# A pair's check numbers on GpSimd: in the step of the pair's last threshold instead of four steps later

## The chip, the cores and the metric

The kernel runs on one core of a Trainium2 chip. The metric is the device time of one execution in microseconds (us). The kernel before has a median of 878.46 us; the execution that was profiled took 872.71 us, of which its trace spans 870.8 us.

## The reference

Sparse attention, then a soft mixture of experts, then a two-layer MLP. Only the first part is touched. For each of 4 batches and 8 heads (sequence 576, head dimension 64) a row of scores keeps its 32 largest values:

```python
scores = scale * np.matmul(q, k.transpose(0, 1, 3, 2))
kth = np.partition(scores, -top_k, axis=-1)[..., -top_k:-top_k + 1]
mask = scores >= kth
scores = np.where(mask, scores, -1000000000.0)
scores = scores - np.max(scores, axis=-1, keepdims=True)
attn = np.exp(scores)
attn = attn / (np.sum(attn, axis=-1, keepdims=True) + 1e-09)
return np.matmul(attn, v).astype(np.float32)
```

Its output is the input of the experts, and theirs of the MLP. In the kernel these are three stages one behind the other.

## The kernel before

**Pairs, tiles and steps.** Two heads make a pair, 16 pairs in all, numbered i from 0. A pair has 9 tiles of 128 rows of scores. A step (`step(m)`) works on two tiles, so a pair lasts 4.5 steps and the stage 72 steps; odd pairs begin in the middle of a step. All engines run the stage in an order written by hand: the string `ORDER` lists tokens, each token takes the next entry of its list, and what a step leaves in its lists is issued at its end in the order `t u U H L a p q r c w e v d m D Z`.

**What a step does.** TensorE computes the scores of step m+2 (token a, L223), ScalarE copies them to the tile x (c, L433). VectorE halves the rows of step m+1 with maxima and minima (`tree1`, token t: L238, L239, L240), and GpSimd does the missing minima as two integer operations (u and U: L246, L250). VectorE takes the 32 largest values of each row of step m by four rounds of the eight largest (`tree2`, token d: L260 and L264 three times, L267 at the end). They go into `m8`, in the trace called m: one tile for a pair, 9 x 32 values in each partition, from a pool of two buffers. So the first L260 of pair i+2 writes where pair i's values were, and must wait until every reader of pair i's tile is through. ScalarE makes a penalty R from the threshold (r, L280), TensorE adds it to the transposed scores (w, L315, L316, L320), ScalarE takes the exponentials E (e, L321), and TensorE multiplies them with the values one step later (v, L326). Row sums, reciprocals rc (L340, VectorE) and the normalised tile xl (L345, ScalarE) follow. GpSimd adds the logits of a head (`add_logits`, token l, L361 or L363), and for each coming pair it makes the low parts of q and of k (`split_lo`, token L, L161, the tiles rawq and rawk), one of them in each of two successive steps.

**The check numbers.** The halving can lose one of the 32. So for every row three of the values are compared with the 32nd (the tile cert, L465), and at the end of attention the least of all differences decides whether the program is run once more without halving. In the kernel before, L465 stands in `ending`, token l, four steps after the step with the pair's last tile and behind the addition of the logits of the pair's second head. GpSimd runs its queue in order.

Of the kernel before, what the change touches and what calls it, by code (L numbers as in the profile page):

```python
# [18 lines left out]
ALU = mybir.AluOpType  # L19
# [70 lines left out]
class Attention:  # L90
# [324 lines left out]
    def run(self, between=None):  # L415
        nc = self.nc
# [3 lines left out]
        Ds, X, Fs, m8, xls, avs, RR, ended, mxs, exs = {}, {}, {}, {}, {}, {}, {}, {}, {}, {}  # L420
# [6 lines left out]
        def at(m, token, f):  # L427
            todo[max(m, -2 if token == "Z" else -1)].append((token, f))

        def copy(m, ps, u, hf):  # L430
            if m not in X:
                X[m] = self.tree.tile([128, 2, 576], F32, name="x", bufs=XBUFS)
            nc.scalar.copy(X[m][:, u, 288 * hf : 288 * hf + 288], ps)  # L433

        def relu(n):
            m, t = m8[seq[n][0]], seq[n][1]
            if n < 2 * M - 2:
                R = RR[seq[n]] = self.w3.tile([128, 576], BF16, name="R", bufs=RB)
                self.relu(R, X[n // 2][:, n % 2], m, t)
            else:  # L440

                if not spare:
                    spare.append(self.w2.tile([128, 5, 2, 97], F32, name="V").rearrange("p a b c -> p (a b c)").bitcast(BF16))
                R = RR[seq[n]] = spare[0][:, 576 * (n % 2) : 576 * (n % 2) + 576]
                nc.vector.tensor_scalar(R, X[n // 2][:, n % 2], m[:, t, 31:32], None, ALU.is_lt)

        def values(ex, i, g, slot):

            h = g[0]
            if i not in xls:  # L450
                xls[i] = self.w3.tile([128, 5, 2, 96], F32, name="xl", bufs=XL)
                nc.gpsimd.memset(xls[i][96:128, 2:5], -1e30)
            if (i, h) not in avs:
                avs[i, h] = self.pA.tile([128, 5, 97], F32, name="av")
            self.values(slot, ex, Ds[i]["V"], h, avs[i, h])

        def ending(i, h):

            if (i, h) != (npairs - 1, 1):
                self.add_logits(i, h, xls[i])  # L460
            if h == 0:
                return
            if self.fast:

                nc.gpsimd.tensor_tensor(self.k.cert[:, i], m8[i].rearrange("p t (j e) -> p t j e", e=8)[:, :, 0:3, 7],  # L465
                                        m8[i][:, :, 31:32].to_broadcast([128, 9, 3]), op=ALU.subtract)
            if i % NPAIR == NPAIR - 1:
                sides["x"][0].append((0, self.route(i // NPAIR, [xls[i - 3 + p] for p in range(NPAIR)])))

        def side(name, m, engine):  # L470

            wait, now = sides[name]
            if not now and wait and wait[0][0] <= m:
                g = wait.pop(0)[1]
                now += [g, next(g)]
            if now and engine in (now[1], None):
                now[1] = next(now[0], "")
                if not now[1]:
                    now.clear()

        def step(m):
            nonlocal idle
            if m == M:
                idle = self.pS.tile([128, 288], F32, name="s")
            q = collections.defaultdict(list, carry)
            carry.clear()

            def add(token, f):
                q[token].append(f)

            if 0 <= m + 2 < M:
                scored = []
                for u in range(2):
                    for hf in range(2):
                        add("a", lambda n=seq[2 * m + 4 + u], u=u, hf=hf: scored.append((self.scores(*n, hf), u, hf)))
                        add("c", lambda: copy(m + 2, *scored.pop(0)))
            if 0 <= m + 1 < M:
                up = self.tree1(X[m + 1], m < 0)
                add("t", lambda: Fs.update({m + 1: next(up)}))
                add("u", lambda: next(up, None))  # L500
                add("U", lambda: next(up, None))
            for n in (2 * m - 2, 2 * m - 1):
                if 0 <= n < 2 * M:
                    add("r", lambda n=n: relu(n))
            if m - 1 in ended:

                i, g = ended[m - 1]
                ex, pms, exps = [], [], []
                exs[m - 1] = ex
                add("p", lambda: pms.append(self.maxima_rows(g, mxs.pop(m - 1))))  # L510
                add("q", lambda: self.maxima_copy(g, pms.pop()))

                def weights(cs):
                    if not ex:
                        ex.append(self.w2.tile([128, 5, 320], F32, name="E"))
                    exps.append(self.weights(i, g, {u: RR[i, u] for u in g[1]}, ex[0], cs))

                for cs in [[0, 1], [2, 3], [4]] if g[4] == 256 else [[0], [1], [2], [3], [4]]:
                    add("w", lambda cs=cs: weights(cs))
                    add("e", lambda: exps.pop(0)())  # L520
            if m - 2 in ended:

                iv, gv = ended[m - 2]
                for slot in IN_GROUP[gv[4]]:
                    add("v", lambda slot=slot: values(exs[m - 2][0], iv, gv, slot))
                if gv[1][-1] in (4, 8):

                    key, rs, rc = (iv, gv[0]), [], []
                    at(m + 1, "s", lambda: rs.append(self.sums(avs[key], key[1], m > M)))
                    at(m + 1, "i", lambda: rc.append(self.recip(rs[0])))  # L530
                    if m > M:
                        at(m + 1, "i", lambda: self.last_logits(avs[key], rc[0], iv))
                    for t in range(5):
                        at(m + 1, "n", lambda t=t: self.normalize(avs[key], rc[0], xls[key[0]], key[1], t))
                    at(m + 2, "l", lambda: ending(*key))
            if m in ended:
                add("m", lambda: mxs.update({m: self.maxima(m8[ended[m][0]], ended[m][1])}))
            if 0 <= m < M:
                ms = []
                for n in (2 * m, 2 * m + 1):  # L540
                    i_, t = seq[n]
                    if t == 0:
                        m8[i_] = self.w2.tile([128, 9, 32], F32, name="m8")
                    ms.append(m8[i_][:, t])
                tr = self.tree2(Fs.pop(m), ms)
                for _ in range(5):
                    add("d", lambda: next(tr, None))
            for token, f in todo.pop(m, []):
                add(token, f)
            for name in (ORDER if m < M else END).split():  # L550
                if name[0] == "k":

                    for _ in range(int(name[1:])):
                        self.nc.tensor.matmul(idle[:, :256], self.k.idn.bitcast(BF16)[:, :128], self.k.idn.bitcast(BF16), start=True, stop=True)
                elif name[0] in sides:
                    side(name[0], m, name[1])
                elif q[name]:
                    q[name].pop(0)()
            for name in "t u U H L a p q r c w e v d m D Z".split():
                while q[name]:  # L560
                    q[name].pop(0)()
            carry.update({name: fs for name, fs in q.items() if fs})
            if between:
                between(m)
# [18 lines left out]
        with self.tc.manual_schedule(engines={ENG.Activation, ENG.PE, ENG.DVE, ENG.Pool, ENG.SP}):  # L583
# [17 lines left out]
            for m in range(-2, M + 4):  # L601
                step(m)
# [450 lines left out]
```

## Time and profile before

| | |
|---|---|
| median of the runs | 878.46 us (fastest 878.17) |
| the profiled execution | 872.71 us, span 870.8 us |
| busy, share of the span | TensorE 88%, VectorE 85%, ScalarE 68%, GpSimd 48% |
| steps of attention in full run | about 35 to 505 us |
| tail of attention, experts | about 505 to 600 us |
| MLP | about 600 to 871 us |

Busy shares are means over three stages with different limits, and a busy TensorE includes matmuls whose ends are modelled. For a change in one stage, the idle time of each engine inside that stage and what ended it tell more than the shares.

### The profile page before, as it was taken

How to read it: one execution, taken by the hardware profiler on the slowest of the kernel's cores; microseconds unless marked ns; L12 is line 12 of the kernel's file. 1: busy time of each engine (PE TensorE's matmuls, PEld its weight loads, DVE VectorE, ACT ScalarE, POOL GpSimd, SP SyncE). 2: the span in 40 equal slices, each digit the busy share in tenths (PEclk: the TensorE clock that was granted, in tenths of full speed). 3: DMA queues.
4: the chain of work that ended last, by engine and by line, in shares of the span. 5: the costliest groups of instructions: out<-in, count | busy, mean ns of one | idle time of the engine just before them, and what ended most of it. 6: DMA issues, size and time to landing. Idle time of an engine off the chain costs nothing.

```text
span 870.8 us, 17807 instructions
## 1 busy us (share of the span) xinstructions
PE 766.0 (88%) x6222; PEld 659.8 (76%) x6222; DVE 736.7 (85%) x2206; ACT 593.8 (68%) x1330; POOL 419.0 (48%) x475
## 2 busy tenths in 40 slices
PE   4689999989989999899999898895479889999997
PEld 2588898889878889798898776672357667888885
DVE  3998988998898998889988946768989998868773
ACT  3478888878877888778778753227665755676562
POOL 3466566556576556565556520002635453433432
PEclk7699999999999999999999999996889999999999
DMA  3626446634654665365153468991130000001011
GB/s 86 160 71 169 120 106 162 165 83 130 160 125 117 178 143 146 104 165 124 41 131 87 149 236 334 404 383 49 57 136 1 1 36 37 1 0 73 1 38 41
DMA packets 60985, 103.41 MB, mean 119 GB/s; under 512 B 24853, under 2 KB 24853, under 8 KB 59861
## 3 DMA queue, kind: packets, MB, share of 16 engines
q1 hardware_dynamic: 60884, 102.18, 40.3%
q8 instruction: 51, 0.84, 0.4%
q14 instruction: 50, 0.40, 0.2%
HBM read 69.86 MB, written 4.72 MB: 86 GB/s over the span
## 4 chain that ended last, share of the span: by engine, by line
PE 39%; DVE 38%; ACT 7%; POOL 5%; issue 5%; DMA 4%; SPq 1%; POOLq 0%; DVEq 0%; ACTq 0%
DVE f L264 7%; PE av L326 7%; DVE m L260 6%; PE o L971 5%; PE o L972 5%; PE o L973 5%; DVE m L267 4%; DVE h L238 4%; DVE hs L944 3%; DVE e L937 2%; DVE f L239 2%; PE s L223 2%; DVE hs L935 2%; PE st L315 2%; DVE f L240 2%
## 5 line engine op out<-in xcount | busy, mean ns | idle before, releaser
L326 PE MATMUL av<-V,E 112*107 112x97 f32 (+5 forms) x1600 | 190.9, 267 | 1.6 <-ACT E L321 1.6
L246 POOL TENSOR_TENSOR f<-x,h 128x576 int32<-128x576 int32 x71 | 100.5, 1416 | 167.2 <-DVE f L240 68.1
L326 PEld LDWEIGHTS av<-V,E 112*107 112x107 f32 (+5 forms) x1600 | 177.2, 181 | 1.8 <-ACT E L321 1.7
L1007 ACT ACTIVATE e<-e 128x768 f32<-128x768 f32 (+2 forms) x168 | 115.3, 744 | 74.8 <-DVE e L937 74.5
L321 ACT ACTIVATE E<-st 128x320 f32<-128x320 f32 (+2 forms) x256 | 117.5, 487 | 55.4 <-PE st L320 52.4
L947 POOL TENSOR_TENSOR gl<-hs,gh 128x768 fp32r<-128x768 f32 (+2 forms) x56 | 92.6, 1654 | 128.0 <-DVE gh L946 123.8
L260 DVE MAX8 m<-f 128x8 f32<-128x100 f32 (+2 forms) x432 | 119.4, 316 | 33.3 <-POOL cert L465 33.3
L264 DVE MATCH_REPLACE8 f<-m,f 128x100 f32<-128x100 f32 (+2 forms) x432 | 131.5, 312 | 0.0
L315 PE MATMUL st<-Qs,Ka 128*128 128x256 f32 (+1 forms) x320 | 110.2, 352 | 14.5 <-ACT E L321 14.1
L223 PE MATMUL s<-Ka,Qs 128*128 128x288 f32 x320 | 104.8, 341 | 18.0 <-ACT Ka L186 9.9
L972 PE MATMUL o<-w,gl 128*128 128x512 f32 x288 | 117.7, 409 | 0.8 <-POOL gl L947 0.8
L971 PE MATMUL o<-w,gh 128*128 128x512 f32 x288 | 118.0, 410 | 0.0
L973 PE MATMUL o<-w,gh 128*128 128x512 f32 x288 | 117.0, 406 | 0.0
L280 ACT ACTIVATE R<-x,m 128x576 bf16<-128x576 f32 x142 | 111.7, 794 | 2.2 <-DVE m L267 0.6
L433 ACT COPY x<-s 128x288 f32<-128x288 f32 x288 | 101.7, 407 | 8.1 <-PE s L223 7.2
L250 POOL TENSOR_TENSOR f<-f,x 128x576 int32<-128x576 int32 x71 | 100.7, 1418 | 0.6
L267 DVE MAX8 m<-f 128x8 f32<-128x576 f32 x144 | 100.8, 742 | 0.0
L316 PE MATMUL st<-Qb,Kb 128*128 128x256 f32 (+1 forms) x320 | 93.9, 302 | 3.5 <-ACT Qb L305 3.5
L223 PE MATMUL s<-Kb,Qs 96*128 96x288 f32 x320 | 94.0, 308 | 0.3 <-DVE Kb L189 0.3
L320 PE MATMUL st<-dm,R 128*128 128x128 bf16 (+1 forms) x790 | 88.9, 219 | 5.1 <-ACT R L280 4.2
L223 PEld LDWEIGHTS s<-Ka,Qs 128*128 128x128 f32 x320 | 63.7, 199 | 20.4 <-ACT Ka L186 10.4
L315 PEld LDWEIGHTS st<-Qs,Ka 128*128 128x128 f32 x320 | 61.8, 193 | 19.5 <-ACT E L321 16.9
(152 smaller groups left out, 1424.9 us busy)
## 6 DMA issues: line engine op xcount, KB each, us to landing
w<-in_w SPq DMA_DIRECT2D x30, 1024.0 KB, 7.6
Ka<-hik SPq DMA_DIRECT2D x62, 144.0 KB, 2.6
raw<-in_w_in SPq DMA_DIRECT2D x8, 1024.0 KB, 8.3
raw<-in_w_out SPq DMA_DIRECT2D x8, 1024.0 KB, 5.0
rawq<-in_qT SPq DMA_DIRECT2D x16, 288.0 KB, 3.6
rawk<-in_kT SPq DMA_DIRECT2D x16, 288.0 KB, 3.3
vT<-in_vT SPq DMA_DIRECT2D x16, 288.0 KB, 4.2
Qb<-Qs SPq DMA_DIRECT2D x32, 144.0 KB, 2.6
```

Of the source, the lines that this page charges most:

```text
L223: nc.tensor.matmul(ps, q, k, start=n == 0, stop=n == len(todo) - 1)
L260: V.max(M[j][u], f[:, u, part])
L264: V.match_replace(out=f[:, u, part], in_to_replace=M[j][u], in_values=f[:, u, part], imm_value=NEG)
L267: V.max(M[3][u], f[:, u])
L280: self.nc.scalar.activation(R, x, AF.Relu, bias=m8[:, t, 31:32], scale=-1.0)
L315: T.matmul(ps[:, j], self.Ka[z][:, ks], self.Qs[z][:, 64 * h + q0 : 64 * h + q0 + n], start=j == 0, stop=False, skip_group_check=True)
L321: return lambda: nc.scalar.activation(ex[:, cs[0] : cs[0] + len(cs), :n], ps, AF.Exp, scale=SCALE)
L326: self.nc.tensor.matmul(av[:w, j], ex[:k, c, o : o + w], V[:k, c, h], start=c == 0 and j == 2 * h, stop=c == 4, skip_group_check=True)
L971: T.matmul(ps, gh[:, c, r : r + 128], w[0], start=f == 0, stop=False)
L972: T.matmul(ps, gl[:, c, r : r + 128], w[0], start=False, stop=False)
L973: T.matmul(ps, gh[:, c, r : r + 128], w[1], start=False, stop=f == 15)
L1007: nc.scalar.activation(mid[i][1], mid[i][1], func, **kw)
```

## The change

L465 moves out of `ending` into a function of its own, and that is called under the token U in the step where the pair's last tile (tile 8) gets its values. Its list of U holds the second integer operation L250 ahead of it, so it is issued at the end of the step, behind L250. The operation, its operands and its result are the same.

```diff
             if h == 0:
                 return
-            if self.fast:
-
-                nc.gpsimd.tensor_tensor(self.k.cert[:, i], m8[i].rearrange("p t (j e) -> p t j e", e=8)[:, :, 0:3, 7],
-                                        m8[i][:, :, 31:32].to_broadcast([128, 9, 3]), op=ALU.subtract)
             if i % NPAIR == NPAIR - 1:
                 sides["x"][0].append((0, self.route(i // NPAIR, [xls[i - 3 + p] for p in range(NPAIR)])))
+
+        def certify(i):
+
+            nc.gpsimd.tensor_tensor(self.k.cert[:, i], m8[i].rearrange("p t (j e) -> p t j e", e=8)[:, :, 0:3, 7],
+                                    m8[i][:, :, 31:32].to_broadcast([128, 9, 3]), op=ALU.subtract)
@@
             if m in ended:
                 add("m", lambda: mxs.update({m: self.maxima(m8[ended[m][0]], ended[m][1])}))
+                if self.fast and ended[m][1][1][-1] == 8:
+                    add("U", lambda: certify(ended[m][0]))
```

The first place is GpSimd's queue in the step where pair 4's check numbers stood; m_2070 is the tile m of pair 4, m_2460 that of pair 5. Before:

```order
L246 TENSOR_TENSOR f<-x,h 128x2x288
L291 TENSOR_SCALAR mx<-col 128x2
L292 TENSOR_TENSOR mx<-col,mx 128x2
L250 TENSOR_TENSOR f<-f,x 128x2x288
L363 TENSOR_TENSOR L<-xl 128x160
L465 TENSOR_TENSOR cert<-m_2070 128x27
L161 TENSOR_TENSOR rawq<-rawq,hiq 128x576
L246 TENSOR_TENSOR f<-x,h 128x2x288
```

And of the change:

```order
L246 TENSOR_TENSOR f<-x,h 128x2x288
L291 TENSOR_SCALAR mx<-col 128x2
L292 TENSOR_TENSOR mx<-col,mx 128x2
L250 TENSOR_TENSOR f<-f,x 128x2x288
L363 TENSOR_TENSOR L<-xl 128x160
L468 TENSOR_TENSOR cert<-m_2460 128x27
L161 TENSOR_TENSOR rawq<-rawq,hiq 128x576
L246 TENSOR_TENSOR f<-x,h 128x2x288
```

A cert still stands here, but it is that of pair 5, whose last tile falls into this step; pair 4's has gone four steps ahead. The second place is that earlier step on GpSimd, where pair 4 gets its last values (m_2071 is now the name of its tile). Before:

```order
L246 TENSOR_TENSOR f<-x,h 128x2x288
L291 TENSOR_SCALAR mx<-col 128x2
L292 TENSOR_TENSOR mx<-col,mx 128x2
L250 TENSOR_TENSOR f<-f,x 128x2x288
L161 TENSOR_TENSOR rawq<-rawq,hiq 128x576
L246 TENSOR_TENSOR f<-x,h 128x2x288
```

And of the change:

```order
L246 TENSOR_TENSOR f<-x,h 128x2x288
L291 TENSOR_SCALAR mx<-col 128x2
L292 TENSOR_TENSOR mx<-col,mx 128x2
L250 TENSOR_TENSOR f<-f,x 128x2x288
L468 TENSOR_TENSOR cert<-m_2071 128x27
L161 TENSOR_TENSOR rawq<-rawq,hiq 128x576
L246 TENSOR_TENSOR f<-x,h 128x2x288
```

The check numbers now stand ahead of the subtraction rawq of that step. The third place is VectorE, with what each instruction waits for, where pair 6 (m_3061, now m_3062) begins in the buffer of pair 4. Before:

```order
L267 MAX m_2460<-f 128x8 [waits Pool_49]
L267 MAX m_2460<-f 128x8
L290 TENSOR_REDUCE col<-m_2460 128x2
L260 MAX m_3061<-f 128x8 [waits DVE_49,Pool_49]
L260 MAX m_3061<-f 128x8
L264 MATCH_REPLACE f<-m_3061,f 128x100 [waits DVE_49] x2
```

And of the change:

```order
L267 MAX m_2460<-f 128x8 [waits Pool_49]
L267 MAX m_2460<-f 128x8
L290 TENSOR_REDUCE col<-m_2460 128x2
L260 MAX m_3062<-f 128x8 [waits DVE_49]
L260 MAX m_3062<-f 128x8
L264 MATCH_REPLACE f<-m_3062,f 128x100 [waits DVE_49] x2
```

The first L260 of the pair no longer waits for GpSimd (Pool). The orders of TensorE, ScalarE, VectorE and of the DMA queue are otherwise as before.

## Rows read from the trace of the kernel before

**Rows 1.** The page: busy time of each engine; the chain that ended last.

```profile
PE 766.0 (88%) x6222; PEld 659.8 (76%) x6222; DVE 736.7 (85%) x2206; ACT 593.8 (68%) x1330; POOL 419.0 (48%) x475
...
PE 39%; DVE 38%; ACT 7%; POOL 5%; issue 5%; DMA 4%; SPq 1%; POOLq 0%; DVEq 0%; ACTq 0%
```

**Rows 2.** Stretches: length, busy us of PE, PEld, DVE, ACT, POOL; clock, DMA.

```profile
35.00:505.00 470.00, 435.74 (x3997) 400.51 (x3997) 433.60 (x1721) 380.38 (x1012) 282.63 (x360) 0.99 0.50 128
80.00:120.00 40.00, 38.16 (x322) 35.03 (x321) 34.56 (x141) 30.88 (x83) 24.44 (x32) 0.91 0.48 130
```

**Rows 3.** Waits of VectorE, 35 to 505: total us, times, longest us.

```profile
DVE m L260 <- POOL cert L465: 33.3, 14, 2.7
DVE rc L340 <- ACT rs L335: 0.5, 1, 0.5
```

**Rows 4.** Timeline of GpSimd where pair 4's check numbers stand: start, us.

```profile
204.24 1.41 POOL L250 TENSOR_TENSOR f<-f,x 128x576 int32<-128x576 int32 x1
205.61 0.53 POOL L363 TENSOR_TENSOR L<-xl 128x160 f32<-128x160 f32 x1
206.09 0.27 POOL L465 TENSOR_TENSOR cert<-m 128x27 f32<-128x27 f32 x1
206.32 1.42 POOL L161 TENSOR_TENSOR rawq<-rawq,hiq 128x576 f32<-128x576 f32 x1
```

**Rows 5.** Timeline of VectorE at the same place.

```profile
206.40 0.43 DVE L260 MAX8 m<-f 128x8 f32<-128x100 f32 x2 [2.73 <-POOL cert L465]
...
209.57 0.75 DVE L238 TENSOR_TENSOR h<-x 128x576 f32<-128x576 f32 x1
```

**Rows 6.** Timeline of VectorE: the wait for an odd pair, two kinds.

```profile
171.95 0.27 DVE L260 MAX8 m<-f 128x8 f32<-128x100 f32 x1 [1.33 <-POOL cert L465]
...
233.75 0.27 DVE L260 MAX8 m<-f 128x8 f32<-128x100 f32 x1 [2.56 <-POOL cert L465]
```

**Rows 7.** Check numbers over the run: ns min/median/max, first and last start.

```profile
L465 POOL TENSOR_TENSOR cert<-m x16: 255/261/274, 83.8 to 519.1; 128x27 f32<-128x27 f32 x16
```

**Rows 8.** Timeline of GpSimd: two subtractions of low parts.

```profile
64.91 1.42 POOL L161 TENSOR_TENSOR rawk<-rawk,hik 128x576 f32<-128x576 f32 x1
...
119.46 1.43 POOL L161 TENSOR_TENSOR rawq<-rawq,hiq 128x576 f32<-128x576 f32 x1
```

**Rows 9.** Timeline of VectorE: the halving beside those two.

```profile
65.67 1.27 DVE L238 TENSOR_TENSOR h<-x 128x576 f32<-128x576 f32 x1
...
120.56 0.94 DVE L238 TENSOR_TENSOR h<-x 128x576 f32<-128x576 f32 x1
```

**Rows 10.** Waits of TensorE, 35 to 505.

```profile
PE st L315 <- ACT E L321: 14.1, 10, 2.5
PE m L301 <- POOL mx L292: 8.4, 10, 2.5
PE st L320 <- ACT R L280: 3.9, 15, 0.3
```

**Rows 11.** Timeline of VectorE, then ScalarE, then TensorE, 356 to 370.

```profile
356.83 0.27 DVE L260 MAX8 m<-f 128x8 f32<-128x100 f32 x1 [2.55 <-POOL cert L465]
...
367.62 0.18 DVE L340 RECIPROCAL rc<-rs 128x5 f32<-128x5 f32 x1
...
367.84 0.34 ACT L345 ACTIVATE xl<-av,rc 128x96 f32<-128x96 f32 x1 [2.83 <-DVE rc L340]
...
369.62 0.38 PE L315 MATMUL st<-Qs,Ka 128*128 128x256 f32 x1 [2.51 <-ACT E L321]
```

**Rows 12.** Timeline of ScalarE and VectorE: a copy of scores, the halving that reads it.

```profile
396.81 0.99 ACT L433 COPY x<-s 128x288 f32<-128x288 f32 x3
...
399.65 0.92 DVE L238 TENSOR_TENSOR h<-x 128x576 f32<-128x576 f32 x1
```

**Rows 13.** Timeline of TensorE: ten values matmuls at the two clock levels.

```profile
365.98 1.13 PE L326 MATMUL av<-V,E 112*107 112x97 f32 x10
...
371.38 2.28 PE L326 MATMUL av<-V,E 112*128 112x97 f32 x10
```

## The prediction

> **What bounds the kernel now.** I read the page first. TensorE and VectorE are both above 80% busy and share the chain that ended last almost evenly [rows 1], so over the whole span neither is the bound. The change touches attention alone, so I then read the stretch of full steps, 35 to 505 us: TensorE is busy 435.7, VectorE 433.6 and ScalarE 380.4 of 470 us [rows 2]. Two engines have the same 35 us left. The waits tell which of them is driven. VectorE waits for one thing only: 14 times for the check numbers, 33.3 us in all; everything else adds 0.5 us [rows 3]. So VectorE never ran out of scores, and outside these 14 waits it is gapless. The 14 are the pairs 2 to 15, each waiting for the cert of the pair two before it.
>
> The place of the wait shows the mechanism. GpSimd finishes L250, adds the logits, takes the check numbers at 206.09 to 206.36 [rows 4], and VectorE's first L260 of the next pair starts at 206.40 after 2.73 us of idling [rows 5]. The cert itself takes 0.26 us [rows 7]; what VectorE waits for is the queue ahead of it. All 7 even pairs (their certs stand behind a pair with L363 or L361 and before a rawq) look like this place and cost about 2.73. The 7 odd pairs come in two kinds, 2.56 and 1.33 us [rows 6]; the short one is the end of a batch, where VectorE adds the logits itself: 3 of the 7. 7 x 2.73 + 4 x 2.56 + 3 x 1.33 = 33.3, the sum of the waits row.
>
> **What the change removes.** The new cert stands one pair-length of 4.5 steps ahead of the L260 that needs it, and that L260 has lost its wait for GpSimd. The whole wait goes: -33.3 us on VectorE. The other readers of the old tile m are the penalties R on ScalarE and the column maxima on VectorE, which run within about a step of the threshold; no row shows VectorE waiting for them, and I take nothing for them.
>
> **What it adds.** The cert in its new place waits for nothing new: GpSimd reaches it behind L250, when the step's last values are long written. GpSimd has 470 - 283 = 187 us free in the stretch, so 16 x 0.26 us on its own queue are covered. What is not covered is whom its work now meets. When L161 on GpSimd (two float inputs) runs at the time of VectorE's L238 (two inputs too), L238 is late: L161 ends at 66.33 and L238 at 66.94 after 1.27 us; in the other place L161 ends at 120.89 and L238 at 121.50 after 0.94 us [rows 8, 9]. Undisturbed it takes 0.75 [rows 5]. In both, L238 ends 0.61 us after L161 ends. So it makes almost no progress until L161 is through. The Trainium skill states such a rule, in "SBUF — State Buffer", section "Who interferes with whom": a VectorE instruction with two SBUF inputs contends with a GpSimd instruction that reads SBUF. It speaks against this change, since the wait kept the two apart; the rows above agree with it.
>
> Now the even places. In rows 4, L161 runs from 206.32 to 207.74. Today L238 comes at 209.57, long after it. Without the 2.73 us it would come at 206.84, in the middle of L161, and the cert ahead of L161 does not vanish from this step, since the next pair's stands there now. By the 0.61 above L238 ends at 208.35 instead of 207.59: 0.76 us lost. There are 7 such places: +5.3 us. At the odd places no L161 follows the old cert, and nothing is lost. In the own step of each even pair, the cert now pushes rawq back by 0.26 us, and L238 there already runs into rawq (the 0.94 us row); it ends 0.26 later, 7 times: +1.8 us. Bounds for both: nothing, if L161 and L238 slip apart, and the full 1.42 us of an L161 at all 14, 20 us, if L238 came just as L161 starts. I take the value by the nearest rows.
>
> VectorE alone would thus gain 33.3 - 5.3 - 1.8 = 26.2 us.
>
> **Whether TensorE and ScalarE follow.** The stretch would be 470 - 26 = 444 us long, against 435.7 us of busy TensorE: 98%. That only works if TensorE's own waits shrink. They are mostly VectorE's stall passed on. The largest kind, 14.1 us, is for exponentials [rows 10]; rows 11 show where it comes from: VectorE loses 2.55 at 356.83, reaches the reciprocal rc at 367.62, ScalarE has waited 2.83 us for it, its exponentials behind that are late, and TensorE waits 2.51. Move VectorE earlier and this goes too. The 8.4 us for mx hang on VectorE's column maxima likewise. The 3.9 us for R are ScalarE's own latency and stay.
>
> Slack is thin all the same. At 399.65 VectorE's halving reads scores whose copy ended at 397.80, 1.85 us before [rows 12]. The removed wait just ahead of it is a net 2.0 us. So VectorE would come some 0.15 us early there, and a little more late in the stage, as the lead that two buffers of scores give is used up once. I take 0.3 us for each of 7 two-pair periods, 2 us. Bounds: 0, or 12 us, which is rival one.
>
> **Sum.** 26.2 - 2 = 24.2 us. The profiled execution would go from 872.7 to 848.5, its span from 870.8 to 846.6. The median is 5.7 us above the profiled execution; I take the same difference off it: 878.5 - 24.2 = 854.3, rounded 854. After attention nothing changes: the loads of the experts are issued from the last steps on, so they move with the end of attention.
>
> **Rivals.**
> *One: TensorE and ScalarE take over.* VectorE then waits for scores (L238 for the copy L433) where it waited for cert. For it: 98% busy, and the thin slack. Against: in the whole stretch VectorE never waited for scores. If only TensorE's 14.1 us for exponentials dissolve, the gain is 14: 864.
> *Two: the whole 33.3 us come through*, because L161 is not met or TensorE's matmuls wait less all along: 845. Against it stand the two collisions in rows 9.
> *Three, the other side: TensorE's clock.* At 1.2 GHz ten value matmuls take 2.28 us instead of 1.13 [rows 13]. From 80 to 120 us the granted clock was 0.91, some 7 of 40 us at the lower level [rows 2], and the slow ten at 371.38 come right behind TensorE's wait of 2.51 us [rows 11, 13]. If the new rhythm brought more falls, each us at that level would cost TensorE half a us. To end over 2% slower (17.6 us) it has to eat the 24 us too: 42 us, or 84 us more at the lower level, where now the 470 us hold some 9 (0.99). TensorE waits less after the change, so this is unlikely: 900 us at that point.
> *Four: no effect*, because another reader of m is as late as cert was. The order shows that the wait for GpSimd is gone, and VectorE's other wait in the stretch is 0.5 us. 878.
>
> **How the numbers follow.** Forecast 0.62 (its own range 849 to 860), rival one 0.19, rival two 0.13, rival three 0.03, rival four 0.03. About 2% is what a measurement of this kernel can tell from no change, so faster means under 861. The forecast gives 0.60 of its 0.62, rival two all, rival one 0.02: faster 0.75. The rest of one and of the forecast, and rival four, are within 2%: 0.22. Slower 0.03. The range 846 to 866 leaves out half of rival two's cases, the upper third of one, and three and four.
>
> **What would show it.** In the profile after, VectorE's wait for cert should be gone from the waits, and its first L260 of each pair should follow the L290 or L267 ahead of it without a gap. At the even places L238 should take about 1.5 us instead of 0.75, with L161 beside it, 7 times; in the own steps of even pairs about 1.2. TensorE's wait for E should fall from 14 us to a few, and ScalarE's for rc with it. VectorE should show small waits of L238 for the copy L433, 2 us in all. I am wrong if these are 10 us or more (rival one), or if L238 stays at 0.75 at the even places (rival two), or if the granted clock of 35 to 480 us is well below 0.99 (rival three).

## The result, and the profile after

The median goes from 878.32 to 852.38 us (runs of 849.5 to 856.29): 0.9711 of the time before, with a 95% interval of 0.9662 to 0.976, so 26 us or 3% faster. One of the four runs of before took 2466.95 us, and the ratio leaves it out. A second, longer measurement of the same kernel (`e5_again` below) gave 0.9724 [0.9702, 0.9746]. The profiled execution took 856.29 us with a span of 854.4, against 872.71 and 870.8: a difference of 16.4 us. The profiled execution of before is faster than the median of its kernel, that of after slower, and so the two differences do not agree; this matters below.

The page after, busy time of the engines and shares of the chain that ended last, to be set against [rows 1]:

```profile
PE 762.4 (89%) x6222; PEld 657.3 (77%) x6222; DVE 742.8 (87%) x2206; ACT 592.0 (69%) x1330; POOL 414.5 (49%) x475
...
PE 45%; DVE 30%; ACT 12%; DMA 5%; issue 4%; SPq 2%; POOL 1%; DVEq 0%; POOLq 0%; ACTq 0%
```

The work is the same, the span shorter. GpSimd has left the chain (5% to 1%). TensorE and ScalarE took what it and VectorE gave up.

Waits of VectorE after, 35 to 490 us (total us, times, longest us), against [rows 3]:

```profile
DVE rc L340 <- ACT rs L335: 12.9, 7, 5.4
```

The 14 waits for cert, 33.3 us, are all gone. A wait that was 0.5 us before has become 12.9: the reciprocal rc waits for ScalarE's row sums rs, which are read from TensorE's product av. Behind this window, at the end of attention, the last rc waits 8.3 us, much as before (7.8).

Waits of TensorE after in the same stretch, against [rows 10]:

```profile
PE st L320 <- ACT R L280: 3.8, 15, 0.3
...
PE m L301 <- POOL mx L292: 1.8, 1, 1.8
...
PE av L326 <- ACT E L321: 1.6, 1, 1.6
PE st L315 <- ACT E L321: 1.5, 3, 1.1
```

TensorE's wait for exponentials fell from 14.1 to 3.1 us (1.5 and 1.6), that for mx from 8.4 to 1.8; that for R stayed (3.9 and 3.8). ScalarE's waits show the same; two kinds of them before, then the one for rc after:

```profile
ACT xl L345 <- DVE rc L340: 23.2, 19, 2.8
...
ACT hiq L158 <- issue: 1.9, 1, 1.9
```

```profile
ACT xl L345 <- DVE rc L340: 7.3, 12, 1.2
```

The wait of hiq with no instruction as releaser stands in both, with 1.9 us; it comes back below.

Next the collision. An even place is a step in which an even pair's check numbers stood before the change; there are 7. First GpSimd's and VectorE's timeline at the even place of [rows 4, 5], some 7 us earlier in the execution; then an own step of an even pair (the one in which it gets its last values), the place of the second of [rows 8, 9]. Columns: start, us.

```profile
199.45 1.42 POOL L161 TENSOR_TENSOR rawq<-rawq,hiq 128x576 f32<-128x576 f32 x1
...
199.91 1.57 DVE L238 TENSOR_TENSOR h<-x 128x576 f32<-128x576 f32 x1
...
115.57 1.42 POOL L161 TENSOR_TENSOR rawq<-rawq,hiq 128x576 f32<-128x576 f32 x1
...
116.47 1.13 DVE L238 TENSOR_TENSOR h<-x 128x576 f32<-128x576 f32 x1
```

L238 now starts inside L161 and ends 0.61 us after it (201.48 against 200.87, and 117.60 against 116.99). It takes 1.57 us where it took 0.75, and 1.57 to 1.62 at all 7 even places. In the own steps only 4 such meetings are seen, with 1.13 to 1.15 us. Over the stage its 69 halvings cost 61.1 us instead of 54.6, in the groups by line of before, then of after:

```profile
L238 DVE TENSOR_TENSOR h<-x 128x576 f32<-128x576 f32 x69 | 54.6, 792 | 0.0
```

```profile
L238 DVE TENSOR_TENSOR h<-x 128x576 f32<-128x576 f32 x69 | 61.1, 886 | 0.0
```

So VectorE's account in this execution is 33.3 us of waits removed, 6.5 us of slower halvings, and 12.4 us of new waits for rs (12.9 less 0.5): 14.4 us. Measured from its L238 of step 3 to that of step 71, the stage went from 459.6 us (41.13 to 500.69) to 444.5 (41.32 to 485.79): 15.1 us. What comes behind that took 370.1 us and then 368.6.

Where the 12.9 us come from is seen in two stretches: the whole one, against [rows 2], and one in which TensorE's clock fell (length, busy us of PE, PEld, DVE, ACT, POOL; granted clock, DMA).

```profile
35.00:480.00 445.00, 427.54 (x3916) 393.81 (x3916) 429.53 (x1681) 370.37 (x991) 275.71 (x351) 0.98 0.51 132
198.00:205.00 7.00, 7.00 (x37) 6.60 (x38) 4.31 (x14) 1.35 (x3) 4.27 (x5) 0.51 0.12 28
```

A second one like it, 259 to 266 us, has a clock of 0.53. The first in the timelines of TensorE, ScalarE and VectorE, and VectorE's wait behind the second:

```profile
197.97 2.37 PE L210 MATMUL m<-phi,vT 128*128 128x64 f32 x10 [1.40 <-DMA vT<-in_vT]
...
201.08 2.10 PE L326 MATMUL av<-V,E 112*107 112x97 f32 x10
...
201.31 0.44 ACT L321 ACTIVATE E<-st 128x320 f32<-128x320 f32 x1 [3.82 <-PE st L320]
...
207.76 0.19 DVE L340 RECIPROCAL rc<-rs 128x5 f32<-128x5 f32 x1 [5.42 <-ACT rs L335]
...
269.62 0.19 DVE L340 RECIPROCAL rc<-rs 128x5 f32<-128x5 f32 x1 [5.33 <-ACT rs L335]
```

TensorE waits 1.40 us for a transfer, runs the next 7 us at 1.2 GHz (clock 0.51), ten value matmuls take 2.10 instead of 1.13 [rows 13], ScalarE waits 3.82 us for its next transposed scores, and VectorE 5.42 us for the row sums. Two such places make 10.75 of the 12.9 us; the other five waits, 0.34 to 0.62 us each, together make 2.1.

### The profile page after: what moved, and what is told of

Its sections match the earlier page's. It is cut to its first block, busy times and chain, and to the rows that moved or that the text cites. A ratio compares the mean times of both kernels' runs of the same rounds, so it can differ in the third digit from the quotient of the medians.

```text
span 854.4 us, 17813 instructions
## 1 busy us (share of the span) xinstructions
PE 762.4 (89%) x6222; PEld 657.3 (77%) x6222; DVE 742.8 (87%) x2206; ACT 592.0 (69%) x1330; POOL 414.5 (49%) x475
## 4 chain that ended last, share of the span: by engine, by line
PE 45%; DVE 30%; ACT 12%; DMA 5%; issue 4%; SPq 2%; POOL 1%; DVEq 0%; POOLq 0%; ACTq 0%
PE av L326 8%; PE o L975 6%; PE o L974 6%; PE o L976 6%; DVE f L264 5%; ACT R L280 4%; DVE m L267 4%; DVE m L260 4%; DVE h L238 3%; PE st L320 3%; PE st L315 3%; PE s L223 2%; DVE e L940 2%; PE st L316 2%; ACT x L433 2%
## 5 line engine op out<-in xcount | busy, mean ns | idle before, releaser
L260 DVE MAX8 m<-f 128x8 f32<-128x100 f32 (+2 forms) x432 | 118.4, 315 | 0.0
L974 PE MATMUL o<-w,gh 128*128 128x512 f32 x288 | 116.7, 405 | 0.0
L976 PE MATMUL o<-w,gh 128*128 128x512 f32 x288 | 115.9, 402 | 0.0
L250 POOL TENSOR_TENSOR f<-f,x 128x576 int32<-128x576 int32 x71 | 100.5, 1416 | 0.6
L938 DVE COPY hs<-h 128x768 f32<-128x768 f32 (+2 forms) x56 | 46.9, 838 | 30.6 <-PE h L936 30.4
```

Source lines behind the costliest of these rows:

```text
L260: V.max(M[j][u], f[:, u, part])
L974: T.matmul(ps, gh[:, c, r : r + 128], w[0], start=f == 0, stop=False)
L976: T.matmul(ps, gh[:, c, r : r + 128], w[1], start=False, stop=f == 15)
```

## The experiments

Each ratio is against the kernel before, run on the same chip. The open questions were three: whether the 33.3 us are 14 separate gains, whether the halving's loss counts, and what the waits for rs are.

### Half of the pairs at a time

Only even pairs take their check numbers early; odd ones do so at the old place, in `ending`:

```diff
             if h == 0:
                 return
+            if self.fast and i % 2 != 0:
+                certify(i)
@@
-                if self.fast and ended[m][1][1][-1] == 8:
+                if self.fast and ended[m][1][1][-1] == 8 and ended[m][0] % 2 == 0:
```

> Only the even pairs' check numbers move; the odd pairs' stay four steps later. Theory (each wait counts by itself, each meeting of L161 and L238 takes its part back): VectorE loses its 7 long waits for cert (2.73 us each, 19.1) and keeps the 7 odd ones (14.2). At the places where the even certs stood, L238 meets rawq, but with no cert ahead of it any more: about 1.35 us instead of 0.75, 7 x 0.6 = 4.2 back; in the even pairs' own steps 7 x 0.2 = 1.4 back. Net 13.5 us: 878 to 865. Rival (TensorE takes over and sets the pace): with half of the waits gone TensorE already bounds the stage, so this alone gives nearly what the whole change gave, 852 to 856, with VectorE waiting for ScalarE or TensorE instead.

Measured: 869.87 us, 0.9881 [0.9826, 0.9936], 10.5 us faster than before (5.6 to 15.3 by the interval). VectorE's waits:

```profile
DVE m L260 <- POOL cert L470: 14.1, 7, 2.6
DVE rc L340 <- ACT rs L335: 11.0, 9, 2.5
```

The 14.1 us of the odd pairs stay, the 19.2 us of the even ones are gone, L238 takes 1.37 us at the even place near 207 us, and waits for rs appear. The mirror image, with only odd pairs early (`% 2 != 1` and `% 2 == 1` in the two lines):

> Only the odd pairs' check numbers move. Theory: the 7 odd waits (4 x 2.56 and 3 x 1.33, 14.2 us) go, the 7 even ones stay at 2.73 and keep rawq and L238 apart, so L238 stays at 0.75 there. Net 14 us: 878 to 864, and with the run of the even pairs alone (13.5) the two add up to the 26 us of the whole change. Rival (TensorE sets the pace): each half alone gives more than half, the two gains add up to well over 26, and this one lies at 852 to 858.

Measured: 862.44 us, 0.9846 [0.9783, 0.9909], 13.5 us (8.0 to 19.1). Its four runs are 858.07, 862.37, 862.51 and 871.98 us, and the last of them weighs on the ratio: by the medians the gain is 17.1 us. VectorE's waits:

```profile
DVE m L260 <- POOL cert L470: 19.1, 7, 2.8
DVE rc L340 <- ACT rs L335: 1.6, 1, 1.6
```

The odd half removes 14.2 us of waits and 13.5 to 17 come through; no halving is slowed (54.6 us, as before), and hardly a wait for rs appears. The even half removes 19.2 and 10.5 come through. Added up they give 24.0 us by the ratios and 26.7 by the medians, against 24.2 for the whole in `e5_again` (0.0276 x 877.61). The times, each good to some 5 us, fit waits that count by themselves; they rule out that either half alone gives nearly the whole. That what is lost is lost at the even places is seen in the traces: the slower halvings and 11.0 us of waits for rs are in the even half (3.1 us of these waits, at 62 and 89 us, behind a fall of the clock from 44 to 55), 1.6 us in the odd one.

### Another place within the window, and the collision taken away

The check numbers two steps later, still ahead of the L260 that needs their buffer:

```diff
-                    add("U", lambda: certify(ended[m][0]))
+                    at(m + 2, "U", lambda: certify(ended[m][0]))
```

> The check numbers of all pairs are taken two steps after the step of the last threshold, in steps with no rawq or rawk behind them; still two and a half steps ahead of the L260 that needs the buffer. Theory (the wait is gone wherever the cert stands early enough; a cert ahead of rawq lengthens the meeting with L238 by its 0.26 us): no wait of VectorE for cert; L238 at the odd pairs' own steps 1.35 instead of 1.61 and in the even pairs' own steps 0.94 instead of 1.14; 7 x 0.26 + 7 x 0.2 = 3.2 us less on VectorE than the change, 849. Rival (TensorE sets the pace after the change): what VectorE saves comes back as waits for ScalarE's row sums, 852.

Measured: 855.23 us, 0.973 [0.9685, 0.9775], the time of the change. Its L238 took 59.3 us, its longest wait for rs was 2.8 us, and its profiled execution, 849.46 us, had no stretch at 1.2 GHz between 75 and 475 us. Within some 4 us the place in the window doesn't matter: what counted was to be out from behind the logits. The 849 us of the expectation were missed. Where L238 got 0.2 us shorter at an even place, the wait for rs behind it got 0.2 us longer (0.34, 0.34 and 0.34 in the profile of the change, 0.56, 0.54 and 0.57 here), as its rival said.

Then, on top of that, the logits at the even places two steps later, so that L161 comes earlier there and no longer meets L238:

```diff
-                    at(m + 2, "l", lambda: ending(*key))
+                    at(m + (4 if iv % 2 == 0 and gv[0] else 2), "l", lambda: ending(*key))
```

> As the run with the check numbers two steps later, and the logits of an even pair's second head are added two steps later as well, so that nothing but L250 stands ahead of rawq. Theory: L238 beside rawq falls from 1.61 to about 0.94 us at 7 places and from 1.14 to 0.94 at 7 others, 7 x 0.67 + 7 x 0.2 = 6.1 us less on VectorE than the change, 846. Rival (TensorE sets the pace after the change): VectorE's waits for the row sums grow by as much, 852.

Measured: 854.78 us, 0.9729 [0.9687, 0.9771]. Waits of VectorE, and an even place in its timeline:

```profile
DVE rc L340 <- ACT rs L335: 12.6, 8, 3.1
```

```profile
202.15 0.90 DVE L238 TENSOR_TENSOR h<-x 128x576 f32<-128x576 f32 x1
...
205.23 0.19 DVE L340 RECIPROCAL rc<-rs 128x5 f32<-128x5 f32 x1 [1.31 <-ACT rs L335]
```

The edit did what it was to do: L238 takes 0.90 here, and 56.0 us over the stage where the change has 61.1. Nothing of it shows in the time, by the ratio 0.4 us above `e5_again`, good to some 4 us. At four even places the waits for rs were 0.34, 0.62, 0.34 and 0.50 us in the profile of the change; here they are 1.06, 1.50, 1.04 and 1.26 (the longest, 3.1, has another source, shown below). VectorE arrives earlier and waits longer: at the even places rs sets the pace, not VectorE. The theory that the halving's loss can be won back fell here.

### The change again

> The change once more, beside the next three. In its profile two of VectorE's waits for the row sums rs were 5.4 us, each where the granted clock fell to 1.2 GHz for 6.8 us right after TensorE had waited (for vT, for E); the other five were 0.3 to 0.6. Theory (those two are the clock's, not the change's): where this profile has no such stretch, the waits for rs sum to some 2 to 4 us, and where it has some, there is one long wait for each. Rival: the long waits come at the same two places whatever the clock does, and the sum is again about 13. Time 852 to 856 either way.

Measured: 853.42 us, 0.9724 [0.9702, 0.9746]. Its profiled execution took 853.81, with a span of 852.0. Waits of VectorE, then the long one among them, with what is ahead of it on the DMA queue (SPq), ScalarE and TensorE:

```profile
DVE rc L340 <- ACT rs L335: 9.5, 8, 3.6
```

```profile
242.00 0.58 SPq L658 DMA_DIRECT2D w<-in_w  x1
243.24 0.59 SPq L173 DMA_DIRECT2D Qs<-hiq  x1
...
254.46 0.67 ACT L158 CAST hiq<-rawq 128x576 fp32r<-128x576 f32 x1 [2.16 <-issue]
...
255.52 0.87 PE L326 MATMUL av<-V,E 112*107 112x97 f32 x4 [1.78 <-ACT E L321]
...
265.72 0.19 DVE L340 RECIPROCAL rc<-rs 128x5 f32<-128x5 f32 x1 [3.64 <-ACT rs L335]
```

```profile
256.00:260.00 4.00, 4.00 (x24) 3.77 (x24) 4.00 (x21) 3.27 (x8) 3.92 (x7) 0.57 0.82 167
75.00:475.00 400.00, 386.34 (x3600) 355.76 (x3599) 389.25 (x1527) 338.97 (x909) 251.34 (x322) 1.00 0.53 135
```

The fall near 198 us is not here: TensorE waits 0.23 us for its transfer vT there, not 1.40, and VectorE waits 1.02 us for rs. The long wait near 265 is here again, smaller. Ahead of it a weight transfer of 1 MB stands on the DMA queue just before the copies of the coming pair's Qs and Ka. ScalarE's hiq then waits 2.16 us with no instruction as releaser, its exponentials are late, TensorE waits 1.78, and its clock falls for the next 4 us.

The other seven waits make 5.9 us. Two of them are 1.22 us at 62.37 and 1.60 at 89.52, behind one more fall: from 44 to 55 us the granted clock is 0.53, and 1.00 in the profile of the change. It shows in the third of 40 equal slices of the span, first of the change, then of this execution:

```profile
PEclk7699999998998999999999999996789999999999
PEclk7779999999999999999999999996699999999999
```

Ahead of it TensorE waits 2.12 us for mx, where it waited 1.76 in the profile of the change. In that profile there is no wait at 62 us and one of 0.34 at 87. `e11_quarters` below has the fall and both waits again (1.11 and 1.59 us); `e3_two_later`, without the fall, has none at 62 and 0.56 at 87. The five waits that are left make 3.0 us and don't come behind a fall.

### Is it the amount of TensorE's work?

If TensorE, busy in 96% of the stretch (427.54 of 445 us), were the limit behind rs, less work on it would shorten the time. So the change with the low part of k left out of the scores, one of two matmuls per group of scores:

```diff
-        todo = [(self.Qs[z][:r, q : q + 128], K[z][:r, 288 * hf : 288 * hf + 288]) for z, q in ops for K, r in ((self.Ka, 128), (self.Kb, 96))]
+        todo = [(self.Qs[z][:r, q : q + 128], K[z][:r, 288 * hf : 288 * hf + 288]) for z, q in ops for K, r in ((self.Ka, 128),)]
```

> The change, with the low part of k left out of the scores (20 of TensorE's matmuls in each pair, about 0.135 us from one to the next, 2.7 us a pair); the scores are a little coarser, nothing else is left out. Theory (after the change TensorE sets the pace where pairs of even number used to wait): VectorE's waits for the row sums go to under 1 us, and the time falls by about what they were without clock falls and somewhat more at the end of attention, 3 to 8 us: 845 to 850. Rival (VectorE sets the pace, TensorE has room): no change, 852 to 855. Second rival (ScalarE is what is late): the waits stay.

Measured: 862.64 us, 0.9841 [0.9823, 0.986]: 9 us slower than the change by the medians, with less to do; 845 to 850 were expected. Two stretches, and TensorE ahead of one of the falls:

```profile
75.00:475.00 400.00, 370.46 (x3283) 329.84 (x3280) 388.61 (x1511) 333.93 (x896) 248.19 (x319) 0.95 0.52 135
460.00:469.00 9.00, 8.44 (x51) 7.38 (x50) 8.93 (x33) 5.68 (x14) 4.01 (x6) 0.62 0.13 23
```

```profile
457.80 0.40 PE L223 MATMUL s<-Ka,Qs 128*128 128x288 f32 x1 [0.28 <-ACT x L433]
458.41 0.31 PE L301 MATMUL m<-idr,mx 128*2 128x128 f32 x3 [0.21 <-POOL mx L292]
...
459.63 0.40 PE L223 MATMUL s<-Ka,Qs 128*128 128x288 f32 x1 [0.57 <-ACT x L433]
...
460.74 0.42 PE L316 MATMUL st<-Qb,Kb 128*128 128x320 f32 x1 [0.56 <-ACT Qb L305]
461.15 2.23 PE L210 MATMUL m<-phi,vT 128*128 128x64 f32 x10
```

TensorE's busy time in the 400 us fell from 386.34 to 370.46, its granted clock from 1.00 to 0.95: some 40 us at 1.2 GHz. In its four runs the clock over the whole program is 0.920 to 0.926, in those of `e5_again` 0.951 to 0.959. No wait ahead of this fall is longer than 0.57 us, but there are four in 3 us. The next ten matmuls of L210 take 2.23 us. The lighter TensorE finishes, waits briefly and often, and loses its clock. How the 9 us come from that is not seen in the profiled executions, which are 5.9 us apart (859.7 and 853.81): from VectorE's L238 of step 3 to that of step 71 they took 444.2 and 441.7 us.

Two more kernels with the same matmul left out: the one of `e4_apart`, and the kernel before.

> The run with check numbers and logits moved apart from rawq, again without the low part of k in the scores. Theory (TensorE's pace took what L238 gained there, the waits for rs having gone from 0.3 to 0.6 us each to 1.0 to 1.5): with TensorE lighter they vanish, and L238's 5 us now count: 5 us under the run of the change without the low part, 840 to 845. Rival (L238 beside rawq costs nothing that matters): the same time as that run.

> The kernel before, again without the low part of k in the scores. Theory (before the change the wait for cert sets the pace and TensorE does not): the 14 waits stay at 33 us, TensorE only waits more, and the time stays within 1% of the kernel before, 870 to 880. Rival (TensorE already shares the bound before): it falls by over 2%, to 860 or less.

Measured: 863.62 us, 0.9849 [0.9832, 0.9866], with L238 back at 56.1 us and 15.1 us of waits for rs; and 873.92 us, 0.9948 [0.9921, 0.9974], with these waits of VectorE and this stretch:

```profile
DVE m L260 <- POOL cert L465: 33.1, 14, 2.7
DVE rc L340 <- ACT rs L335: 3.2, 1, 3.2
```

```profile
75.00:475.00 400.00, 362.83 (x3157) 323.95 (x3156) 363.88 (x1452) 323.35 (x868) 239.86 (x307) 0.93 0.51 129
```

The first missed its expectation by 20 us, and its clock had fallen too; it decides nothing. The second tells more: in the kernel before, a TensorE that lost its clock still more often (0.93, against 0.99 in the profile of before) left VectorE's 14 waits for cert as they were and came with one wait for rs of 3.2 us; from step 3 to step 71 it took 462.0 us, against 459.6. The median is 3.7 us below that of before, where the change's rose by 9.2. That the waits for cert covered what TensorE lost, and that this cover is gone after the change, fits the medians; the stretches of the profiled executions, both some 2.5 us longer, don't show it.

To tell the clock from any other reason, the idle time was filled: `e6_light` with ten matmuls of 256 columns into a spare buffer, which nobody reads, eight times in the stage, in steps that have no values matmuls of their own.

```diff
+        def fill():
+            pf = self.pT.tile([128, 1, 320], F32, name="st")
+            for _ in range(10):
+                nc.tensor.matmul(pf[:, 0, :256], self.k.idn.bitcast(BF16)[:, :128], self.k.idn.bitcast(BF16), start=True, stop=True)
@@
-                add("p", lambda: pms.append(self.maxima_rows(g, mxs.pop(m - 1))))
+                add("p", lambda: (pms.append(self.maxima_rows(g, mxs.pop(m - 1))), 2 < m < M and m - 2 not in ended and fill()))
```

> The change without the low part of k in the scores, as before, but with ten idle matmuls (256 columns, about 0.11 us each) put in once in nine steps, in the step where TensorE's waits stood close together (0.3, 0.2, 0.6, 0.6 us) ahead of six of the seven regular falls to 1.2 GHz. Theory (the lighter kernel lost its time to the clock: 48 us at 1.2 GHz in attention instead of 14): the regular falls go, and the time comes down from 862.6 to 850 to 855, although TensorE now has more to do. Rival (something else in the lighter kernel costs the 9 us, such as ScalarE): the time stays at 860 to 864 whatever the clock shows.

Measured: 854.19 us, 0.9718 [0.9686, 0.9751]. The stretch, and TensorE at the same place:

```profile
75.00:475.00 400.00, 370.11 (x3366) 328.84 (x3364) 387.93 (x1514) 335.77 (x902) 249.20 (x319) 0.98 0.52 135
```

```profile
458.25 1.27 PE L469 MATMUL st<-idn 128*128 128x256 bf16 x10
...
460.85 1.31 PE L210 MATMUL m<-phi,vT 128*128 128x64 f32 x10
```

Work was added, and the time fell by 8.4 us. The ten of L210 take 1.31 us again. Two falls with long waits for rs (2.79 and 4.91 us) remain, the regular ones are gone. So the loss of `e6_light` comes and goes with the clock. That the clock makes it, and not some other effect of the ten matmuls, is the likely reading but isn't shown in full: in the profiled executions the stretch from step 3 to step 71 is only 1.6 us shorter (442.6 against 444.2). The Trainium skill tells of a like case in "TensorE: Matmul & The Clock Gate", section "A second HAM failure mode: psum-queue depth-cycling": in a bf16 kernel, idle times between groups of matmuls that were very short but frequent made the clock go down and up. The trace of `e6_light` agrees with it: waits of 0.21 to 0.57 us, and a clock of 0.95.

The other half of the answer: with the clock mostly kept (0.98) and 16 us less of busy TensorE, the time is that of the change (0.9718 against 0.9724), and the other five waits for rs are still 0.17 to 0.62 us (0.34 to 0.62 in the profile of the change). So the amount of TensorE's work isn't what holds rs back. The same with `e4_apart`'s order:

> As the run above, with check numbers and logits moved apart from rawq: L238 has its 5 us less. Theory (at even places the chain through TensorE and ScalarE to the row sums rs sets the pace, not VectorE): the waits for rs are larger by what L238 lost, and the time equals that of the run above within 2 us. Rival (the clock hid VectorE's gain): 5 us less than the run above.

Measured: 854.88 us, 0.9736 [0.9703, 0.9768], with L238 at 56.3 us and 12.1 us of waits for rs. Again the halving's 5 us turn into waits. It shows place by place: at the five even places other than those two, L238 is 0.69 to 0.72 us shorter than in `e9_light_filled` (0.94 instead of 1.64 at the first), and the wait for rs behind it is 0.67 to 0.81 us longer (1.06 instead of 0.35).

### The transfer ahead of the head's copies

If the fall near 265 us comes from a 1 MB transfer ahead of small copies, smaller transfers should take it away. The 12 weight transfers of 1 MB that fall into attention become 24 of 512 KB, in every second step instead of every fourth:

```diff
-            for n in range(2 * NUNIT):
-                between[8 + 4 * n].append(lambda u=n // 2, c=n % 2: fetch(u, [c]))
+            for n in range(4 * NUNIT):
+                between[8 + 2 * n].append(lambda u=n // 4, c=n % 4: fetch(u, [c], 4))
```

> The change, with the experts' weights fetched during attention in 24 transfers of 512 KB every second step instead of 12 of 1 MB every fourth. Theory (the long wait for rs near 265 us, 3.6 us in the second profile of the change, comes from a 1 MB transfer issued just ahead of the copies of hiq and hik: ScalarE's next hiq waits 1.9 us for them, its exponentials and so TensorE wait, and the clock falls): no wait of hiq over 1 us, no wait of rs over 1.5 us in 100 to 480 us, 848 to 851. Rival (the clock falls by itself): the long wait stays or moves, 853.

Measured: 850.2 us (846.57 to 850.9), 0.9668 [0.9641, 0.9696]. Waits of VectorE and of ScalarE, and the same reciprocal:

```profile
DVE rc L340 <- ACT rs L335: 6.0, 8, 1.6
...
ACT E L321 <- PE st L320: 50.9, 72, 2.7
ACT x L433 <- PE s L223: 6.7, 13, 0.7
ACT xl L345 <- DVE rc L340: 6.2, 10, 1.0
ACT Qb L305 <- PE m L301: 1.1, 1, 1.1
ACT R L280 <- DVE m L267: 0.4, 1, 0.4
```

```profile
262.16 0.19 DVE L340 RECIPROCAL rc<-rs 128x5 f32<-128x5 f32 x1 [0.35 <-ACT rs L335]
```

ScalarE's wait for hiq is gone, the long wait at this place is 0.35 us, and no wait for rs is over 1.6. This beats the change by some 3 to 5 us: the two intervals lie side by side (0.9641 to 0.9696, and 0.9702 to 0.9746), but the shorter first measurement of the change (0.9662 to 0.976) overlaps with it. With `e4_apart`'s order on top:

> Check numbers and logits apart from rawq, and weights in transfers of 512 KB. Theory: as the run above, since the pace at even places is not VectorE's: 848 to 851. Rival (with the transfers spread, VectorE sets the pace): 5 us below the run above, 843 to 846.

Measured: 848.84 us, 0.9671 [0.9644, 0.9698], with L238 at 56.5 us and 8.2 us of waits for rs: the same as `e11_quarters`. For the third time the halving's 5 us don't come through, here with a single fall of the clock after 75 us, from 278 to 282. The three differences of this kind, 0.4, 1.6 and 0.3 us by the ratios and each good to some 4 us, together leave no room for 5.

## Why the prediction was right, and where it wasn't

**The removed wait.** 33.3 us were to go and went. `e1_even` and `e2_odd` show that each half counts, and `e3_two_later` that the place within the window is free. Nothing took the place of cert as a reader of m, so rival four falls.

**The collision.** Foreseen: 1.51 us at the 7 even places and about 1.2 in the own steps, 7.1 us in all. Measured: 1.57 to 1.62 at the 7 even places, 1.13 to 1.15 in only 4 own steps (0.8 us, where 1.8 were foreseen for 7), and 6.5 us in all (6.0 and 0.8, less 0.3 at a place where a meeting got shorter). Here too L238 ended 0.61 us behind L161's end. The rule cited from the Trainium skill ("SBUF — State Buffer", "Who interferes with whom") agrees with all of these rows. Rival two, which needed L238 undisturbed, falls. But the price in the kernel's time is another: three kernels without the collision (`e4_apart`, `e10_apart_light_filled`, `e12_apart_quarters`) were no faster than their counterparts. The 6.5 us on VectorE are real, yet nearly all of them lie where it would otherwise wait for rs.

**The coupling.** This step failed in its place, and the clock made it larger. The prediction took 2 us, as waits of L238 for the copy of the scores. L238 never waits for it in the stretch; the waits are those of rc for rs, 9.0 us net (9.5 less 0.5) in one profiled execution and 12.4 in the other. They have two sources. 2.1 us in the profile of the change, 3.0 in `e5_again` and 3.3 in `e11_quarters` come at even places and not behind a fall of the clock, which is near the 2 us foreseen: row sums stand at the end of a chain that goes back and forth between TensorE and ScalarE (R, Qb, the exponentials, the products), and at the even places VectorE now comes to them before they are ready. The rest, 10.75 us in the first execution and 6.5 in the second (3.6 at 265 us, 2.8 behind the fall at 44), stands behind TensorE at 1.2 GHz, for which the sum had no term. The slack in [rows 12] was the wrong place to look: I looked for VectorE's next input (the scores), and not for its other input, which [rows 3] already listed with 0.5 us. That rs sets the pace is shown; which piece of the chain holds rs back was not tried and stays open.

**TensorE's clock.** Rival three was right in its mechanism and far too large: some 14 us at the lower level between 40 and 480 us of the profile after, not the 84 more that would have decided it. But the argument against it, that TensorE waits less after the change, is only half of it. In the profile of before some 10 us at that level (around 107 and 372 us) brought VectorE no wait for rs; in that of the change 14 us made 10.75 us of its waits. And `e6_light` was 9 us slower, with falls behind waits of TensorE no longer than 0.6 us.

**The forms of rival one.** TensorE's wait for E fell from 14.1 to 3.1 us and ScalarE's for rc from 23.2 to 7.3, as foreseen. So the gain was not held to 14 us, and `e9_light_filled` speaks against the amount of TensorE's work as the bound. Rival one's idea, that another engine now sets the pace, is nevertheless true at the even places, by way of rs.

**The sum.** The median forecast, 854.0, was 1.6 us off. The sum against the profiled execution, 848.5, was 7.8 us off (856.3; 853.8 in the second profile), mostly since the coupling, with the clock in it, cost 9 to 12 us and not 2. The two differ because I took the 5.7 us between the median of before and its profiled execution as a constant: after the change the profiled executions were 3.9 and 0.4 us above the median. So part of the agreement of the median is luck: a coupling term too small by 7 to 10 us, and a kernel before whose ordinary executions lie 0.6 to 12.3 us above the one whose rows I had (873.3 to 885.0 us over 37 runs). The granted clock over the whole program goes with it: 0.952 in the profiled execution, 0.929 to 0.951 in the 37, by and large lower in the longer ones (0.950 at 873.27, 0.931 at 884.99). Whether the clock is the cause, and in which stage, stays open; only one execution of it was profiled. By the medians the kernel gained 24 to 26 us, which is what the removed waits less the slower halvings would give; by the two traces it gained 16 to 19.

## What to carry to other kernels

A short instruction that waits in an in-order queue can stall another engine through a buffer that it still has to read: look at who holds the buffer, not at how long the reading takes, and take the last reader's turn earlier. When such a stall goes, sum what will collide, and then look for the next late input of the engine that was stalled in the waits that are now near zero, since these are the ones that grow. Having less to do can cost an engine its clock, and the kernel time with it. And large transfers queued ahead of small copies that something waits for can start such a wait.

## What was not expected of the hardware

- A halving of 128x576 (two inputs on VectorE) that starts inside a GpSimd subtraction of the same size ends 0.61 us behind that subtraction's end, wherever in it the halving started: it took 0.94, 1.13, 1.27 and 1.57 us in the rows shown, and 0.75 undisturbed.
- TensorE's granted clock fell behind four waits of 0.21 to 0.57 us within 3 us, with no longer one among them (`e6_light`). With half the matmuls of the scores taken away the kernel was 9 us slower, and with ten matmuls that nobody reads, eight times, it was 8.4 faster again (by the medians).
- A weight transfer of 1 MB on the queue ahead of a head's copies made ScalarE wait 1.9 us in the profiled execution of before and 1.95 and 2.16 in those of the change; at 512 KB that wait was gone. A fall of the clock did not always follow: in the profiled execution of before and in `e3_two_later` (2.1 us) the clock stayed.
